# q and k of all but the first half batch transposed by DMA from SBUF to SBUF instead of on TensorE

## The chip, the cores and the metric

One core of one Trainium2 chip. The metric is the device time of one execution in microseconds (us). The kernel before takes 264.52 us (median of 4 runs, 264.51 to 264.59). A run is repeated on the same chip beside runs of the kernel before.

## The reference

A sparse attention (4 batches, 8 heads, 768 positions, head size 64) followed by two products with a gated activation between them:

```python
k_sum = k.reshape(B, H, nb, 32, D).max(axis=3)       # one summary key per block of 32
v_sum = v.reshape(B, H, nb, 32, D).mean(axis=3)
scores_l = where(|i - j| < 16, scale * q @ k.T, -1e9) # a narrow band
scores_s = scale * q @ k_sum.T + log(32)              # and the 24 summaries
a = softmax(concat(scores_l, scores_s)); attn = a @ concat(v, v_sum)
h = x @ w_in                                          # x: 3072 x 512, w_in: 512 x 2048
out = (h * sigmoid(1.702 * h)) @ w_out                # w_out: 2048 x 512
```

## The kernel before

The work runs in eight half batches of 384 positions. Each has a first product (tile `ph`, into `gT`) and a second one (tile `po`). Attention for the next half batch is interleaved with the second product: scores (`ps_s`), values (`ps_av`), the transposition of the result (`ps_x`). The inputs of the next batch are prepared in the odd half batches (u odd), in the first product. Scores need the head dimension on the partitions, so q and k have to be transposed:

```python
def load_k(b, p):                       # two heads p: rows of 768 B (three positions each)
    for half in range(2):
        sp.dma_start(out=t[:, half]..., in_=k[b, 2*p:2*p+2, half*HALF:...].rearrange("h (p r) d -> p h (r d)", r=JH))
def cast_k(eng, p): ...                 # f32 -> bf16 on GpSimd, tile kb, three buffers
def tk(p, s, own=dve):                  # on TensorE: matmul with the identity
    for half in range(2):
        p3 = big[:, half*512:half*512+HALF].rearrange("p (c r) -> p r c", r=JH)   # columns written with a step of 3
        for r in range(JH):
            pe.matmul(out=p3[:, r], lhsT=src[:, half, r]..., rhs=ident, start=True, stop=True)
    # DVE: copy from PSUM into the key tile kx, block maxima ks, 16-column halos
def tq(p, half, e0, e1):                # the same for q: 3 matmuls, two DVE copies into zero-padded qz
    ...
# an odd half batch (u odd): what GpSimd casts for the next batch, and the slots of the first product
todo = {1: [tk(0)], 2: [tk(1)], 4: [vsum(0,1,2)], 5: [vsum(3,4,5), vrows], 6: [tk(2)], 8: [tk(3)],
        9: [tq(0,0)], 11: [tq(1,0)], 12: [tq(2,0)], 14: [tq(3,0)]}
cast_k(pool, 0); cast_k(pool, 1)
for j in range(NJ): cast_v(pool, s, j, 0); cast_v(pool, s, j, 1)     # twelve v casts
cast_k(pool, 2); cast_q(pool, 0, 0)                                  # the fourth k cast follows at slot 2
# an even half batch: tq(p, 1) at slots 3, 6, 9, 12; the next batch's loads are issued in its second product
```

`vsum` sums v by blocks on TensorE from cast v, `vrows` then copies rows within `vw` by six DMAs. Each engine, and SyncE's queue of DMA instructions, works strictly in program order. [...]

The softmax here doesn't subtract the row's maximum and nothing guards it: scores larger than these inputs give would overflow.

## Time and profile before

| | before |
|---|---|
| time | 264.52 us |
| TensorE busy | 89% |
| from one odd half's end to the next | 56.8 us |
| an odd half (31 us) is longer than an even one (26 us) by | 4.8 us, the preparation of the next batch |

How to read such a page: a row of 40 digits is the span in 40 slices, 9 is 90% busy or more; `PEclk` is the granted clock in tenths. TensorE at 9 all along with no waits is the bound. The lines are shown in the prediction below. Lines in order of time have the start and the length in us, the engine, the operation, the tiles written and read, and in brackets how long the engine stood idle before and for whom. `SPq` is SyncE's queue of DMA instructions; its length there is how long the instructions held the queue, not how long the data took to land. A "slot" is one of the sixteen column blocks of the first product.

### The profile page before, as it was taken

How to read it: one execution, taken by the hardware profiler on the slowest of the kernel's cores; microseconds unless marked ns; L12 is line 12 of the kernel's file. 1: busy time of each engine (PE TensorE's matmuls, PEld its weight loads, DVE VectorE, ACT ScalarE, POOL GpSimd, SP SyncE). 2: the span in 40 equal slices, each digit the busy share in tenths (PEclk: the TensorE clock that was granted, in tenths of full speed). 3: DMA queues.
4: the chain of work that ended last, by engine and by line, in shares of the span. 5: the costliest groups of instructions: out<-in, count | busy, mean ns of one | idle time of the engine just before them, and what ended most of it. 6: DMA issues, size and time to landing. Idle time of an engine off the chain costs nothing.

```text
span 263.1 us, 4275 instructions
## 1 busy us (share of the span) xinstructions
PE 234.2 (89%) x1571; PEld 142.0 (54%) x1592; DVE 146.7 (56%) x336; ACT 131.3 (50%) x218; POOL 75.5 (29%) x185
## 2 busy tenths in 40 slices
PE   2543749999998999999989999999989999999994
PEld 1131535656665555655665656566656556555541
DVE  4527471447699483358796754276995745372000
ACT  3524443663644627752646446844446366637711
POOL 8890792735203003840202006820220000000000
PEclk9998555999999999999999999999999999999999
DMA  6969999998432118993150129972130210011012
GB/s 176 227 173 178 306 202 196 196 221 259 171 52 55 40 42 223 229 272 117 42 103 0 42 92 249 261 239 83 22 81 2 81 40 2 9 71 42 0 40 81
DMA packets 52981, 32.34 MB, mean 123 GB/s; under 512 B 26848, under 2 KB 49888, under 8 KB 52960
## 3 DMA queue, kind: packets, MB, share of 16 engines
q1 hardware_dynamic: 48736, 27.88, 41.9%
q0 software_dynamic: 4224, 4.19, 9.7%
q8 instruction: 12, 0.20, 0.3%
q14 instruction: 9, 0.07, 0.1%
HBM read 27.26 MB, written 6.29 MB: 128 GB/s over the span
## 4 chain that ended last, share of the span: by engine, by line
PE 74%; DVE 8%; POOL 6%; ACT 5%; DMA 2%; issue 2%; SPq 1%; ACTq 0%; POOLq 0%
PE po L27 29%; PE ph L27 26%; PE ps_s L27 4%; PE ps_q L27 4%; PE ps_av L27 4%; DVE kx L27 4%; PE ps_x L27 3%; DMA qf<-in_q_dram 2%; PE ps_k L27 2%; DVE ks L27 2%; ACT L27 2%; DVE x_sb L27 2%; PE ps_vs L27 1%; POOL qz L27 1%; POOL vw L27 1%
## 5 line engine op out<-in xcount | busy, mean ns | idle before, releaser
L27 PE MATMUL ph<-xT,w_in_sb 128*128 128x384 bf16 x512 | 97.7, 335 | 0.7 <-ACT gT L27 0.7
L27 PE MATMUL po<-w_out_sb,gT 128*128 128x512 bf16 x363 | 92.5, 379 | 0.8
L27 ACT ACTIVATE gT<-ph 128x384 bf16<-128x384 f32 x128 | 61.6, 490 | 46.3 <-PE ph L27 45.7
L27 PEld LDWEIGHTS <-w_in_sb 128*128 128x128 bf16 x512 | 52.6, 106 | 31.2 <-issue 5.2
L27 PEld LDWEIGHTS <-gT 128*128 128x128 bf16 x384 | 34.6, 97 | 28.0
L27 DVE CAST qz<-ps_q 64x384 bf16<-64x384 f32 x56 | 31.1, 555 | 28.6 <-PE ps_q L27 28.0
L27 POOL CAST qb<-qf 128x384 bf16<-128x384 f32 x32 | 16.1, 513 | 101.5 <-PE ps_q L27 63.6
L27 DVE TENSOR_TENSOR a_sb<-a_sb,mk 128x768 bf16<-128x768 bf16 x32 | 18.4, 575 | 33.8 <-ACT a_sb L27 32.9
L27 ACT ACTIVATE a_sb<-ps_s 128x768 bf16<-128x768 f32 x32 | 25.2, 809 | 23.4 <-PE ps_s L27 23.3
L27 DVE TENSOR_TENSOR x_sb<-ps_av,rc 64x384 bf16<-64x384 f32 x64 | 35.5, 555 | 1.5
L27 ACT ACTIVATE osb<-po 128x512 f32<-128x512 f32 x24 | 14.3, 597 | 41.1 <-PE ps_x L27 23.3
L27 DVE CAST kx<-ps_k 128x768 bf16<-128x768 f32 (+1 forms) x64 | 25.5, 439 | 10.3 <-PE ps_k L27 10.3
L27 POOL CAST vw<-vf 128x512 bf16<-128x512 f32 x42 | 24.6, 620 | 7.5 <-DMA vf<-in_v_dram 7.3
L27 PE MATMUL ps_k<-ident,kb 128*128 128x128 bf16 x96 | 15.5, 351 | 7.6 <-DVE kb L27 3.9
L27 POOL CAST kb<-kf 128x384 bf16<-128x384 f32 x26 | 13.5, 542 | 29.2 <-PE ps_k L27 26.5
L27 ACT ACT_TABLE_LOAD x16 | 20.5, 1283 | 1.1 <-PEq L511 0.8
L27 PE MATMUL ps_q<-ident,qb 128*128 128x128 bf16 x96 | 16.7, 316 | 4.6 <-DVE kx L27 3.4
L27 PE MATMUL ps_s<-qz,kx 128*128 128x128 bf16 x192 | 16.8, 227 | 4.3 <-ACT qz L27 4.3
L27 PEld LDWEIGHTS <-kx 128*128 128x128 bf16 x192 | 13.9, 102 | 10.4 <-issue 4.1
L27 PEld LDWEIGHTS <-a_sb 128*128 128x128 bf16 x192 | 14.4, 102 | 7.7 <-DVE a_sb L27 0.8
L27 PE MATMUL ps_av<-vw,a_sb 128*128 128x130 bf16 x192 | 17.6, 231 | 0.6 <-DVE a_sb L27 0.5
L27 PEld LDWEIGHTS <-kb 128*128 128x128 bf16 x96 | 11.2, 139 | 11.8 <-POOL kb L27 4.4
(42 smaller groups left out, 115.0 us busy)
## 6 DMA issues: line engine op xcount, KB each, us to landing
kf<-in_k_dram SPq DMA_DIRECT2D x32, 192.0 KB, 4.0
vf<-in_v_dram SPq DMA_DIRECT2D x24, 256.0 KB, 5.1
qf<-in_q_dram SPq DMA_DIRECT2D x32, 192.0 KB, 4.2
out_dram<-osb SPq DMA_DIRECT2D x24, 256.0 KB, 2.0
w_in_sb<-in_moe_w_in_dram POOLq DMA_DIRECT2D x4, 512.0 KB, 10.0
w_out_sb<-in_moe_w_out_dram POOLq DMA_DIRECT2D x4, 512.0 KB, 20.5
vw<-vs SPq DMA_DIRECT2D x8, 148.5 KB
vw<-vw SPq DMA_DIRECT2D x8, 99.0 KB, 2.9
```

What stands on the lines that cost most here:

```text
L27: r = f(*a, **kw)
```

## The change

Its intent: take the transpositions off TensorE, which is the bound, and their evacuation off DVE. GpSimd casts k and q to bf16, and the DMA engines transpose from SBUF to SBUF on the way into the key tiles and the zero-padded queries. k and q have to be loaded with positions in partitions in order, hence in 256 B rows.

```diff
+        else:
+            for hh in range(2):          # load_k, load_q of later batches: 256 B rows
+                sp.dma_start(out=t[:, hh]..., in_=k[b, 2 * p + hh].rearrange("(j p) d -> p j d", p=128))
+    qs = [keep.tile([128, JH, 2, 128], BF16, name=f"qs{i}") for i in range(3)]   # zero-padded staging
+    def turn_k(p, s):
+        t = castp.tile([128, NJ, 2, D], BF16, name="kb", tag="kb")               # three buffers
+        pool.tensor_copy(out=t..., in_=raw["k", p]...)
+        for e in range(2):
+            todo_sp.append(lambda e=e: sp.dma_start(out=k4[:, :, e, e * 64:e * 64 + 64],
+                in_=src[e * 64:e * 64 + 64], transpose=True))
+    def turn_q(p, half):
+        t = qs[qn[0] % 3]; qn[0] += 1
+        for hh in range(2):
+            pool.tensor_copy(out=t[:, :, hh, hh * 64:hh * 64 + 64], in_=raw["q", p, half][:, hh])
+        todo_sp.append(lambda: sp.dma_start(out=qz[p][half]..., in_=t..., transpose=True))
+    def rest_k(p, s): ...                # DVE: block maxima and halos, now from the key tile itself
[...]
         if half == 0:
-                cast_q(pool, p, 1)
-                todo[3 + 3 * p] = [lambda p=p: tq(p, 1, dve, dve)]
+                todo[2 + 3 * p] = [lambda p=p: turn_q(p, 1)]
         elif b + 1 < B:
-            [...]  cast_k(pool, 0), cast_k(pool, 1), v casts, cast_k(pool, 2), later cast_k(pool, 3)
+            for p in range(NP):
+                turn_k(p, s)
             for j in range(NJ):
                 cast_v(pool, s, j, 0)
                 cast_v(pool, s, j, 1)
+            todo = {4: [lambda: rest_k(0, s)], 6: [...], 8: [...], 10: [...],
+                    9: [lambda: vsum(s, (0, 1, 2)), lambda: turn_q(0, 0)],
+                    11: [lambda: vsum(s, (3, 4, 5)), lambda: vrows(s), lambda: turn_q(1, 0)],
+                    12: [lambda: turn_q(2, 0)], 13: [lambda: turn_q(3, 0)]}
         for nt in range(NT):
             ff_in(u, nt)
+            if todo_sp:
+                todo_sp.pop(0)()         # one transposing DMA behind each column block
```

## The prediction

> **What bounds the kernel now.** I read the page from the top: busy shares, the 40 slices, the chain that ended last. Then the table of busy times over stages that I cut at the chain's own boundaries, and last the lists in order of time of SyncE, GpSimd and TensorE for one batch.
>
> ```profile
> PE 234.2 (89%) x1571; PEld 142.0 (54%) x1592; DVE 146.7 (56%) x336; ACT 131.3 (50%) x218; POOL 75.5 (29%) x185
> PE   2543749999998999999989999999989999999994
> POOL 8890792735203003840202006820220000000000
> PEclk9998555999999999999999999999999999999999
> DMA  6969999998432118993150129972130210011012
> PE 74%; DVE 8%; POOL 6%; ACT 5%; DMA 2%; issue 2%; SPq 1%; ACTq 0%; POOLq 0%
> ```
>
> After about 40 us TensorE is at 9 in nearly every slice with the clock fully granted: from there on TensorE is the bound, and GpSimd and the DMA engines have bursts once per batch. The kernel runs eight half batches. I call one "even" (first half of a batch) or "odd" (second half); each has a first product (tile ph) and a second (po). In the table by stages (columns: length, then PE, PEld, DVE, ACT and POOL busy) the pair of one batch is:
>
> ```profile
> 98.50:111.00 12.50, 12.34 (x80) 7.74 (x79) 4.80 (x9) 9.11 (x18) 7.27 (x14) 1.00 1.00 219
> 111.00:124.60 13.60, 13.30 (x106) 7.96 (x107) 8.66 (x19) 6.07 (x9) 3.91 (x7) 1.00 0.67 206
> 124.60:141.40 16.80, 16.04 (x109) 10.47 (x107) 14.61 (x33) 8.99 (x17) 3.75 (x8) 1.00 0.26 57
> 141.40:155.30 13.90, 13.60 (x107) 8.09 (x109) 9.28 (x21) 6.17 (x9) 0.14 (x1) 1.00 0.10 39
> ```
>
> PE is busy 12.34 of 12.50 and 16.04 of 16.80: nothing waits long. The period is 12.5 + 13.6 + 16.8 + 13.9 = 56.8 us. The odd first product is 4.3 us longer than the even one because TensorE transposes the next batch's k and q there. How the inputs arrive (lists in order of time: SyncE's queue, then GpSimd):
>
> ```profile
> 99.43 2.00 SPq L27 DMA_DIRECT2D kf<-in_k_dram  x4
> 101.47 6.54 SPq L27 DMA_DIRECT2D vf<-in_v_dram  x6
> 108.11 2.56 SPq L27 DMA_DIRECT2D kf<-in_k_dram  x4
> 110.71 5.69 SPq L27 DMA_DIRECT2D qf<-in_q_dram  x8
> 116.49 8.93 SPq L27 DMA_DIRECT2D out_dram<-osb  x3
> 131.34 2.64 SPq L27 DMA_DIRECT2D vw<-vw  x4
> 134.09 1.71 SPq L27 DMA_DIRECT2D vw<-vs  x2
> ...
> 106.07 7.07 POOL L27 CAST vw<-vf 128x512 bf16<-128x512 f32 x12 [0.69 <-DMA vf<-in_v_dram]
> 126.89 0.51 POOL L27 CAST kb<-kf 128x384 bf16<-128x384 f32 x1 [10.39 <-PE ps_k L27]
> ```
>
> SyncE starts the next batch's loads at 99.43, right after the last output store of the odd half: it runs ahead of TensorE. Its last output store of the even half is out at about 125.4. The v casts are done by 113, long before the sums need them at 129. The last line matters most: the fourth cast of k waited 10.39 us, because the pool of cast buffers has three and the first comes free only when it has been read.
>
> **What the Trainium skill says.** "DMA: Bandwidth & Descriptors", DMA Transpose (X-bar): the plain transpose is issued by SyncE or ScalarE only and writes SBUF; the trace of before has none, so it neither agrees nor disagrees. The same page, Latency and other measured facts: 261 GB/s effective for one transposing kernel. "VectorE: DVE Perf Modes", The three transpose paths: 1309 ns by DMA for 128x128 bf16, 390 ns on TensorE. The trace differs for TensorE: six k transposes take 0.66 us of the chain and three q transposes 0.49, so 0.11 to 0.16 us each. The same DMA page, Specifications: 512 B is the least run for full rate. The trace agrees mildly: v (256 B runs) came at 1.57 MB / 6.54 us = 240 GB/s, q (768 B runs) at 1.57 / 5.69 = 276.
>
> **The change, part by part.**
> Removed from TensorE: per odd half with a next batch 4 x 0.66 (k) + 4 x 0.49 (q) = 4.6 us; per even half 4 x 0.49 = 2.0 us. Three odd and four even: 13.8 + 8.0 = 21.8 us. If nothing new showed, 264.5 - 21.8 is about 243.
> Removed from DVE: 56 casts of 0.555 us (q) and 12 of about 0.9 us (k), some 42 us. Only a few tenths per odd half lie on the chain.
> GpSimd: casts of about the same elements; little changed in amount, much in order (below).
> Loads: k and most of q now come in 256 B rows. 4.7 MB at 240 GB/s is 19.7 us instead of 17.1.
> Added: per batch 8 k transposes (64 x 768) and 8 q transposes (128 x 768) on SyncE's queue. Let T be one q transpose, and half of that for k. An estimate from the trace: 768 rows of 256 B at v's rate of 1.06 ns a row (1.09 us for 1024) is 0.8 us; the page's 261 GB/s gives 0.75. The page's 1.309 us for a sixth of the data gives 7.9, but that figure surely contains the start and the landing of one transfer (a 99 KB copy within SBUF takes 2.9 us to land here). I choose T = 1.6, twice the optimistic value, and think anything from 0.7 to 4 possible.
>
> Now the path, with the odd half's end as time 0. SyncE works in program order, and the program puts four q transposes before the loads. The zero-padded staging tiles are three, so the fourth transpose waits for a first landing and a cast: loads start near 7. They last 20 and end at 27 (the stores end at about 24.5). Only then come the k transposes. The fourth k cast now stands **before** the twelve v casts on GpSimd, and it needs the first cast buffer, hence the first pair's k transposes: 27 + 2 x 0.8 + 3.5 to land behind the loads = 32.1; its cast 33.1; v casts 7.1, so 40.2. Before, the v casts overlapped the loads. TensorE reaches the v sums at about 32 in the odd first product and stalls up to 40.2. Then 0.65 (sums) and four column blocks 2.6: the second product starts at 43.5. The row copies of v (six DMAs, 4.4 us of SyncE's queue) start at about 41.5 and stand before the second q transpose: it lands at 45.9 + 1.6 + 2 = 49.5, while the second group of scores is due at 45.6: 3.9 us more. The half ends at 43.5 + 14.1 + 3.9 = 61.5, against 56.8: about +5 per batch, although TensorE has 6.6 us less to do.
> Sum: the first half batch -2; the first odd half about +4.5, for its loads wait behind q transposes that wait for GpSimd's casts at 39 us, while before they began at 26; two full pairs 2 x 5; the seventh half -2. Together about +10: **274 us**.
>
> **The rivals.** (1) The transposes hide and TensorE stays the bound: about 243. For it: 50% DMA idle time in the slices and the small TensorE waits. Against it: the idle DMA time comes where SyncE's order cannot use it, and the 10.39 us wait for a cast buffer shows the dependency already there. If the v casts are not held up I would be wrong here.
> (2) Transposes at the bandwidth limit, T = 0.8: the loads end near 25, the v casts at 37.5, the half at about 58: +1.5 per batch, 268 in all. So even fast transposes give almost nothing, since the order of the v casts costs what TensorE saves.
> (3) SyncE's queue or the DMA engines become the bound: T = 3 costs some 5.5 us per us of T and batch (four before the loads, two k halves, one q): 274 + 1.4 x 5.5 x 3 = 297; T = 8 would give over 350. For it: 1309 ns for one block on the page. Against it: the same page's bandwidth.
> (4) TensorE's stalls cool its clock: the slices with PEclk 5 lie where it idled early. It would add one or two us per batch; I leave it inside the range.
>
> **Range and chances.** T below 0.7: 15%, to 266; 0.7 to 1.3: 25%, 266 to 272; 1.3 to 2: 25%, 272 to 283; 2 to 4: 20%, to 317; above: 15%. One chance in ten that the cast order costs less than I think moves some weight under 259. Hence 274, range 255 to 320; faster 0.13, same 0.23, slower 0.64. The result is lopsided: a gain is capped at 21.8 us, a loss is not.
>
> **What would show it.** Right: TensorE's matmuls from cast q and k drop from 192 to 36 and its busy time by about 20 us; the v casts of each batch move from the even half into the odd first product, after a GpSimd wait on a DMA; TensorE waits for v casts at the sums (several us) and for q tiles at the second scores; SyncE's loads start some 6 to 7 us after the last odd store; the row copies of v stand between the first and second q transposes. Wrong: TensorE still at 9 in all slices after 40 us (rival 1), or SyncE's queue busy without a pause and transposes taking 3 us or more each (rival 3). What would make the number wrong first is T, then how long the 256 B loads last, then whether the first k transposes really have to wait for all loads to be issued.

## The result, and the profile after

The changed kernel takes 300.03 us (median of 4 runs, 299.28 to 300.79), against 264.52. The ratio is 1.134 (95% interval 1.131 to 1.137). The time lies within the predicted range, but the forecast was +10 us and +35 came.

The page of the changed kernel (busy shares, TensorE, granted clock and DMA by slices, the chain by engine):

```profile
PE 231.7 (78%) x1415; PEld 129.9 (44%) x1436; DVE 113.0 (38%) x268; ACT 131.3 (44%) x218; POOL 74.2 (25%) x199
PE   3544679998066599999658499999568599999995
PEclk9996559999759689999959799999958599999999
DMA  6969999999744506899846614899645513201001
PE 61%; SPq 9%; POOL 9%; DMA 8%; ACT 7%; issue 3%; DVE 1%; POOLq 0%; ACTq 0%
```

TensorE has three holes after 65 us, with slices of 5 to 8 in the clock row beside them: one per odd half that prepares a batch. Its busy time fell by only 2.5 us (234.2 to 231.7) although 156 matmuls have gone. In the pair shown below it fell where the clock was full (even first product, 12.34 to 10.94 us) and not in the odd half (29.6 and 29.7 us), where the clock was 0.87 to 0.89. The chain that ended last now has SyncE's queue, GpSimd and DMA with 26% together, where before they had 9%.

I cut the span at ScalarE's change of function at the end of each half (its table load), which gives lengths that can be compared run by run:

| | first half | first odd | second odd | third odd | each even | span |
|---|---|---|---|---|---|---|
| before | 68.2 | 30.8 | 30.8 | 30.8 | 26.0 | 263.1 |
| after | 67.0 | 48.4 | 41.5 | 42.6 | 24.7 | 298.1 |

The even halves gained 1.3 us each, as work left TensorE. The three odd halves lost 17.6, 10.8 and 11.8. The stages of the pair that answers to the one shown before (same columns):

```profile
114.70:125.80 11.10, 10.94 (x68) 6.47 (x68) 0.36 (x1) 9.02 (x17) 0.64 (x2) 1.00 0.84 153
125.80:139.40 13.60, 13.30 (x104) 7.82 (x105) 8.61 (x19) 6.10 (x8) 2.48 (x3) 1.00 1.31 213
139.40:167.80 28.40, 16.89 (x86) 8.61 (x87) 10.48 (x23) 11.60 (x20) 10.07 (x21) 0.87 0.68 142
167.80:181.00 13.20, 12.83 (x91) 7.39 (x92) 8.03 (x18) 3.62 (x5) 1.94 (x6) 0.89 0.20 59
```

In the third row TensorE is busy 16.89 of 28.40 us, at a granted clock of 0.87. SyncE's queue over this pair (in order of time; the even half begins at 114.8, the odd one at 139.6):

```profile
115.82 6.02 SPq L27 DMA_TRANSPOSE qz<-qs  x4
121.89 2.37 SPq L27 DMA_DIRECT2D kf<-in_k_dram  x4
...
134.97 9.69 SPq L27 DMA_DIRECT2D qf<-in_q_dram  x16
...
146.25 10.37 SPq L27 DMA_TRANSPOSE kx<-kb  x8
158.45 1.21 SPq L27 DMA_TRANSPOSE qz<-qs  x1
159.75 2.61 SPq L27 DMA_DIRECT2D vw<-vw  x4
162.46 1.70 SPq L27 DMA_DIRECT2D vw<-vs  x2
164.26 4.07 SPq L27 DMA_TRANSPOSE qz<-qs  x3
```

The loads begin 7 us after the odd half's end, behind four q transposes; they end at 144.7; eight k transposes hold the queue for 10.4 us; the last three q transposes stand behind the row copies of v. GpSimd in the same odd half:

```profile
150.16 0.83 POOL L27 CAST kb<-kf 128x768 bf16<-128x768 f32 x1 [12.44 <-DMA kx<-kb]
150.93 6.91 POOL L27 CAST vw<-vf 128x512 bf16<-128x512 f32 x12
```

And TensorE:

```profile
151.63 0.58 PE L27 MATMUL ps_vs<-vw,E 128*128 128x512 bf16 x1 [4.97 <-POOL vw L27]
154.30 2.77 PE L27 MATMUL ph<-xT,w_in_sb 128*128 128x384 bf16 x8
...
157.62 2.76 PE L27 MATMUL ph<-xT,w_in_sb 128*128 128x384 bf16 x16
...
167.93 0.80 PE L27 MATMUL ps_s<-qz,kx 128*128 128x128 bf16 x6 [4.79 <-DMA qz<-qs]
168.52 2.98 PE L27 MATMUL po<-w_out_sb,gT 128*128 128x512 bf16 x8
```

The fourth k cast waited 12.44 us for the first k transposes to land, and only then come the v casts. TensorE waits 4.97 us for the first of them, and 4.79 us for the second q tile. After the first wait 8 matmuls of the first product take 2.77 us, as long as 16 of them three microseconds later: the clock was at half.

And the first odd half, which lost most. SyncE's queue in the half before it:

```profile
37.56 13.49 SPq L27 DMA_TRANSPOSE qz<-qs  x4
51.10 4.48 SPq L27 DMA_DIRECT2D kf<-in_k_dram  x4
```

GpSimd meanwhile:

```profile
48.17 0.64 POOL L27 CAST qs<-qf 128x192 bf16<-128x192 f32 x2 [9.51 <-issue]
```

The first batch's four q transposes hold the queue for 13.49 us, because they land 10.5 to 14.9 us after issue while the weights are being loaded, and the fourth has to wait for a staging tile: its cast comes at 48.17. (The profile names no releaser for that cast, "issue"; that it is the first of the three staging tiles follows from the program.) The loads of the second batch start at 51.10; before they started at 26.13. The start overstates the delay, though, for in the kernel before the v loads then stood in the queue for 23.69 us beside the weights:

```profile
28.82 23.69 SPq L27 DMA_DIRECT2D vf<-in_v_dram  x6
```

So the loads ended at 64.0 before and at 75.9 after: 12 us later, not 25.

### The profile page after: what moved, and what is told of

The parts are those of the page before. It is cut to its first block, busy times and chain, and to the rows that moved or that the text cites. A ratio compares the mean times of both kernels' runs of the same rounds, so it can differ in the third digit from the quotient of the medians.

```text
span 298.1 us, 4015 instructions
## 1 busy us (share of the span) xinstructions
PE 231.7 (78%) x1415; PEld 129.9 (44%) x1436; DVE 113.0 (38%) x268; ACT 131.3 (44%) x218; POOL 74.2 (25%) x199
## 3 DMA queue, kind: packets, MB, share of 16 engines
HBM read 27.26 MB, written 6.29 MB: 113 GB/s over the span
## 4 chain that ended last, share of the span: by engine, by line
PE 61%; SPq 9%; POOL 9%; DMA 8%; ACT 7%; issue 3%; DVE 1%; POOLq 0%; ACTq 0%
PE po L27 25%; PE ph L27 23%; SPq L27 9%; POOL vw L27 4%; PE ps_av L27 4%; PE ps_s L27 4%; DMA qz<-qs 4%; PE ps_x L27 3%; ACT L27 3%; DMA kx<-kb 3%; ACT osb L27 2%; DMA qf<-in_q_dram 2%; PE ps_vs L27 2%; ACT gT L27 1%; POOL qz L27 1%
## 5 line engine op out<-in xcount | busy, mean ns | idle before, releaser
L27 PE MATMUL po<-w_out_sb,gT 128*128 128x512 bf16 x363 | 97.6, 395 | 0.8
L27 PE MATMUL ph<-xT,w_in_sb 128*128 128x384 bf16 x512 | 94.0, 341 | 1.1 <-ACT gT L27 1.0
L27 PEld LDWEIGHTS <-gT 128*128 128x128 bf16 x384 | 36.0, 101 | 31.0 <-issue 5.3
L27 POOL CAST qs<-qf 128x192 bf16<-128x192 f32 x56 | 17.5, 353 | 81.0 <-DMA qz<-qs 63.7
L27 POOL CAST kb<-kf 128x768 bf16<-128x768 f32 (+1 forms) x14 | 11.2, 806 | 86.9 <-DMA kf<-in_k_dram 42.4
L27 PE MATMUL ps_vs<-vw,E 128*128 128x512 bf16 x24 | 12.1, 549 | 26.2 <-POOL vw L27 23.1
L27 PEld LDWEIGHTS <-kx 128*128 128x128 bf16 x192 | 14.5, 105 | 27.1 <-issue 21.3
L27 DVE TENSOR_REDUCE ks<-kx 128x24 bf16<-128x768 bf16 x12 | 11.4, 951 | 36.4 <-DMA kx<-kb 36.3
L27 PEld LDWEIGHTS <-E 128*128 128x128 bf16 x24 | 2.9, 121 | 30.2 <-issue 30.0
L27 PE MATMUL ps_x<-ident,x_sb 128*128 128x128 bf16 x96 | 11.2, 229 | 3.2 <-DVE xT L27 3.2
L27 DVE COPY xT<-ps_x 128x384 bf16<-128x384 bf16 x32 | 11.4, 358 | 4.3 <-PE ps_x L27 3.5
```

What stands on the lines that cost most here:

```text
L27: r = f(*a, **kw)
```

## The experiments

The theories. **Order**: what costs is the place of things in two in-order queues, GpSimd's (the v casts behind a k cast that waits for a transpose) and SyncE's (loads behind q transposes, row copies behind k transposes, q transposes behind row copies). **Transpose time**: the transposes in themselves are too slow or fill the DMA engines. **Small rows**: the 256 B loads cost. **Clock**: TensorE's stalls cool it. Lengths of odd halves are of the profiled runs, at the same cuts as above.

**e1: four k cast buffers instead of three.**

```diff
+    kbp = ctx.enter_context(tc.tile_pool(name="kbp", bufs=4))
-        t = castp.tile([128, NJ, 2, D], BF16, name="kb", tag="kb")
+        t = kbp.tile([128, NJ, 2, D], BF16, name="kb4", tag="kb4")
```

> The changed kernel with four k cast buffers instead of three, nothing else. Theory CAST ORDER (my prediction's main step: the fourth k cast holds the v casts back until the first k transposes have landed, and that is what costs): the v casts go back beside the loads, the stall of TensorE at the v sums (5 to 10 us per odd half with a next batch) goes, and the time falls by some 8 us per odd half, to 270-278 us. Theory QUEUE ORDER (the queue of SyncE is the real chain: loads, eight k transposes of 1.25 us, then row copies of v and q transposes, and the cast order only lies in its shadow): the stall moves from the v sums to the first two groups of scores, and the time falls by only 2 to 4 us per odd half, to 288-294 us.

295.45 us, ratio to the kernel before 1.117. TensorE in the second odd half:

```profile
145.18 0.81 PE L27 MATMUL ps_vs<-vw,E 128*128 128x512 bf16 x3
...
158.50 0.80 PE L27 MATMUL ps_s<-qz,kx 128*128 128x128 bf16 x6 [7.10 <-DMA qz<-qs]
...
165.12 0.80 PE L27 MATMUL ps_s<-qz,kx 128*128 128x128 bf16 x6 [4.11 <-DMA qz<-qs]
```

The v sums wait for nothing any more, and the wait stands again before the first scores (7.10 us) and the second (4.11). Only 4.6 us came back, a little less than the queue theory's range allowed (288 to 294): the cast order that my prediction called the main step lies in the shadow of SyncE's queue.

**e2 and e3: one part of the change alone.** In e2 only k goes by DMA; q is loaded, cast and transposed on TensorE as before. In e3 it is the reverse: k as before, with the v casts in their old place.

```diff
 # e2                                              # e3
-    turn_q(p, half) everywhere                    -    turn_k(p, s), rest_k(p, s)
+    cast_q(pool, p, half); tq(p, half, dve, dve)  +    cast_k(pool, p); tk(p, s) at slots 1, 2, 6, 8
                                                   +    vsum at slots 4 and 5, as before
```

> k by DMA as in the change, q of all batches loaded, cast and transposed on TensorE as before. Theory QUEUE/CAST ORDER: the loads start right at the end of the odd half again (no q transposes ahead of them), the k transposes start at the last store of the even half, some 24 us after the odd half's end, the v sums still wait 2 to 4 us and no scores wait for q: 262-268 us. Theory TRANSPOSE TIME (the 24 k transposes and their packets cost in themselves, about half of the loss): about 280 us.

277.69 us, ratio 1.050; the odd halves take 34.9 to 35.2 us. A miss for the order theory's numbers; it lies near the rival's "about 280". One new wait, which neither theory had, makes up nearly all of the loss (12.2 us in the three odd halves), on TensorE in the second odd half:

```profile
140.96 0.82 PE L27 MATMUL ps_q<-ident,qb 128*128 128x128 bf16 x3 [4.08 <-POOL qb L27]
```

The q casts stand on GpSimd behind the v casts, which still stand behind the fourth k cast, so now TensorE waits for a cast q.

> q by DMA as in the change, k loaded, cast and transposed on TensorE as before, so the v casts run beside the loads as before. Theory ORDER: the v sums wait for nothing from the second batch on, the q transposes come after the row copies of v well before the scores; TensorE is rid of 4 x 0.49 us in seven half batches; 250-260 us, with some loss only in the first odd half, where the loads wait for the q transposes of the first batch. Theory TRANSPOSE TIME: q has 28 of the 52 transposes and the larger ones, so half or more of the 35 us loss stays: 280 us or more.

256.32 us, ratio 0.969: faster than the kernel before, with 28 of the 52 transposes, and the larger ones. The odd halves take 33.2, 28.3 and 29.2 us. Only the first shows the late loads. This speaks against transpose time as the cause for q: more than half of the transposes are there and the loss is not. For k it says nothing.

**e4: the kernel before with 256 B loads.** k and q loaded as in the change, transposed on TensorE; each transposing matmul then writes contiguous PSUM columns.

```diff
 # load_k, load_q: two DMAs with 256 B rows in place of one [...]
-  p3 = ps.rearrange("p (c r) -> p r c", r=JH)      # the same for k
+  p3 = ps.rearrange("p (r c) -> p r c", r=JH)
```

> The kernel before, with k and q loaded in 256 B rows as the change does (twice the load instructions for both) and transposed on TensorE; only the order of columns within the transposes differs. Theory ORDER: the loads last 3 to 5 us longer per batch, nothing waits for it, 263-267 us. Rival SMALL ROWS (the smaller rows are what costs): 272 us or more.

259.51 us, ratio 0.981. Unforeseen, this is faster: the odd halves take 29.9 us. It is taken up in e11. Small rows cost nothing that shows here, where nothing waits for the loads. That doesn't clear them in the change: a batch's loads held the queue 17.0 us before (second pair), 24.7 in e4 and 22.8 in the change (of the 5.8 us more, q's loads take 4.0, in 16 instructions instead of 8), and there the transposes stand behind them. No run tests the change with its small rows taken away.

**e5: no q transposes in front of the loads.** The first batch's second-half q goes over TensorE again; those of later batches are issued in the preceding odd half.

```diff
         if half == 0:
-            todo[2 + 3 * p] = [lambda p=p: turn_q(p, 1)]
+            for p in range(NP) if b == 0 else ():
+                cast_q(pool, p, 1); todo[3 + 3 * p] = [lambda p=p: tq(p, 1, dve, dve)]
[...]
+        if half == 1 and b + 1 < B:
+            for p in range(NP): turn_q(p, 1)
```

> The changed kernel with the q transposes of second halves taken from in front of the loads: those of the first batch are done on TensorE again (as in the kernel before), those of later batches are issued in the preceding odd half, behind the first half's. Nothing else. Theory QUEUE ORDER (the loads of a batch wait in SyncE's queue behind four q transposes: 7 us per batch, and some 20 us in the first odd half, where these wait in turn for staging tiles and land late beside the weights): loads start right at the odd half's end, the k transposes start at the even half's last store instead of 6 us later; the first odd half gets 10 to 14 us shorter, the two later ones about 5 us each; 276-283 us. Rival BANDWIDTH (the loads and the weights fill the DMA engines anyway, in whatever order): the first odd half stays within 4 us of its 48 us, 290 us or more.

283.06 us, ratio 1.069. The odd halves take 40.4, 37.0 and 36.6 us: 8.0 less than in the changed kernel in the first, 4.5 and 6.0 in the others. So this place in the queue was worth 17 of the 35 us, just short of the 276 to 283 expected; the first odd half missed the 10 to 14 us expected of it. SyncE's queue in the half before it:

```profile
26.40 4.92 SPq L27 DMA_DIRECT2D kf<-in_k_dram  x4
31.36 25.48 SPq L27 DMA_DIRECT2D vf<-in_v_dram  x6
```

The loads begin 24.7 us earlier than in the change but end only 5.7 us earlier (70.2 against 75.9), as the v loads stand in the queue beside the weights again. So the rival's number (within 4 us of 48) is refuted, but not that what runs beside the weights is slow in whatever order.

**e6: two q transposes in one instruction.**

```diff
-  sp.dma_start(out=qz[p][half]...,  in_=t..., transpose=True)     # 128 x 768
+  sp.dma_start(out=qzp[pp][half]..., in_=t..., transpose=True)    # 128 x 1536, two head pairs
```

> The changed kernel with two q transposes in one instruction (128x1536 instead of twice 128x768), to measure what holds the queue: theory HOLD PER SIZE: one takes 2.4 to 2.6 us of SyncE's queue, twice the 1.24 of a single one. Rival HOLD PER INSTRUCTION: still 1.2 to 1.5 us. By its making the second q of a first half is no longer behind the row copies of v, so the wait of the second scores (4 to 6 us per odd half) should go either way: 284-292 us with the first theory, 280-286 with the second.

289.38 us, ratio 1.093. What one transpose holds of the queue (ns, least, median, most) and how long it takes to land (us), for q of the changed kernel, then its k, then the merged q of e6:

```profile
L27 SPq DMA_TRANSPOSE qz<-qs x28: 1211/1239/5205, 37.6 to 253.4; - x28
DMA to landing us min/median/max: 2.7/3.0/14.9
```

```profile
L27 SPq DMA_TRANSPOSE kx<-kb x24: 1208/1248/1367, 77.9 to 221.5; - x24
DMA to landing us min/median/max: 2.4/2.5/3.1
```

```profile
L27 SPq DMA_TRANSPOSE qz<-qs x14: 1415/1596/7156, 39.2 to 239.4; - x14
DMA to landing us min/median/max: 3.8/4.3/5.3
```

The time lies in the first theory's range, the hold in neither's: half a q (k, 64x768) holds the queue as long as a q (1.25 and 1.24 us), and two q in one hold it 1.6 us. In these shapes the hold is mostly per instruction. Back to back, four q take 5.25 us, which is 786 KB at 150 GB/s; two merged ones take 3.35, which is 235 GB/s; eight k take 10.37 for 786 KB, 76 GB/s. The transposes as the change has them use the queue badly, and k worst.

**e7: idle matmuls in TensorE's waits.**

```diff
+    def warm(ps):                     # ahead of the first v sum and of the second scores of odd halves
+        for i in range(18):
+            pe.matmul(out=ps, lhsT=ident, rhs=w_out_sb[:, i % NT, :], start=True, stop=True)
```

> The changed kernel with 18 matmuls of no use put ahead of the first v sum and ahead of the second group of scores of each odd half, where TensorE stands idle 5 to 10 us; they fill about 4 us of that wait and change nothing else. Theory CLOCK (the clock granted after each stall is lower, and the matmuls that follow run at half speed for 2 to 3 us, which is 3 to 4 us per odd half of the 35 us lost): 289-295 us, granted clock in the odd first products above 0.95. Rival NO CLOCK EFFECT (the chain runs through the queue and the casts, and slower matmuls lie in its shadow): 298 us or more.

292.92 us, ratio 1.106, in the clock theory's range. TensorE at the second scores of the second odd half, after the idle matmuls:

```profile
164.57 0.49 PE L27 MATMUL ps_s<-qz,kx 128*128 128x128 bf16 x6 [1.38 <-DMA qz<-qs]
164.90 1.89 PE L27 MATMUL po<-w_out_sb,gT 128*128 128x512 bf16 x8
```

The same eight matmuls took 2.98 us in the changed kernel. 7.1 us, or 2.4 per odd half, came back though nothing was taken away. The clock was thus a part of the loss and not in another chain's shadow. The granted clock, cut at the start of the second product, rose to 1.00 in the three second products (from 0.86, 0.92 and 0.84). In the first products it rose only to 0.86, 0.92 and 0.92 (from 0.78, 0.84 and 0.76), where above 0.95 was expected: there TensorE still waited for v casts, up to 6.29 us. The Trainium skill, "TensorE: Matmul & The Clock Gate", Part 1, says that the clock halves after an idle window of about 3.4 us; the traces agree for the six long waits of the changed kernel (4.54 to 9.80 us), each followed by slowed matmuls; a wait of 2.5 us in e12 below was followed by slow matmuls once and once not.

**e8: only q by DMA, both chains avoided.** k over TensorE with contiguous writes, q transposes of both halves in the odd half, the first half's ahead of the row copies, none ahead of the loads, four k cast buffers.

```diff
+            cast_k(pool, 0) ... v casts ... cast_k(pool, 2); cast_k(pool, 3)
+            for p in range(NP): turn_q(p, 0)
+            todo = {1: [tk(0, s)], 2: [tk(1, s)], 4: [vsum(s, (0, 1, 2))],
+                    5: [vsum(s, (3, 4, 5)), vrows(s)], 6: [tk(2, s)], 8: [tk(3, s)]}
+            # turn_q(p, 1) at slots 9 to 12
```

> Only q by DMA, k of later batches on TensorE from rows loaded as in e4 (contiguous writes to PSUM), q transposes of both halves issued in the odd half, the first half's ahead of the row copies of v, none ahead of the loads, four k cast buffers. Theory ORDER: no stall of TensorE over 1 us after 40 us; its work falls by 28 - 4 q transposes (24 x 0.49 = 12 us) and by 12 x 0.27 = 3 us for k; 245-252 us, faster than the kernel before and than e3 and e4. Rival TRANSPOSE TIME: the DMA engines are too full and it is no better than e3 (256 us).

250.99 us, ratio 0.948. Its page, busy shares and TensorE by slices:

```profile
PE 224.1 (90%) x1520; PEld 131.3 (53%) x1520; DVE 122.3 (49%) x288; ACT 131.2 (53%) x218; POOL 83.0 (33%) x215
PE   2635576999999899999999999999999999999994
```

From 44 us to the last slice TensorE is at 9, but for one slice of 8: the odd halves take 27.0 us (28.0 the first).

**e9: e2 with four k cast buffers.**

```diff
+    kbp = ctx.enter_context(tc.tile_pool(name="kbp", bufs=4))
-        t = castp.tile(..., name="kb", tag="kb")
+        t = kbp.tile(..., name="kb4", tag="kb4")
```

> e2 (only k by DMA, 277.7 us) with four k cast buffers. In the full change the fourth buffer gave only 5 us, since SyncE's queue lay right behind. Here no q transposes stand in that queue. Theory TWO CHAINS (cast order and queue order each hold TensorE up by themselves, so taking one away helps only where the other is absent): the v casts go back beside the loads, TensorE waits for nothing over 1 us in the odd first products, and the time falls by 20 us to 253-259 us, under the kernel before. Rival TRANSPOSE TIME (k transposes of 10.4 us per batch on the queue cost in themselves): 268 us or more.

268.51 us, ratio 1.013 (0.997 to 1.029). A miss again: 9 us less than e2, where 20 were expected, and the time lies in the rival's range (268 or more). TensorE in the first odd half:

```profile
82.44 0.61 PE L27 MATMUL ps_q<-ident,qb 128*128 128x128 bf16 x3 [3.33 <-DVE qz L27]
```

The v sums wait for nothing, as expected, but now TensorE waits 3.33 us for DVE's copy of a transposed q: DVE, also in order, stands at the block maxima of a key tile that a transpose has still to deliver. That is a third in-order queue on which the change put a wait for a transpose. The lesson for the theory: two chains were too few. With k alone by DMA, order and the 10.4 us that its transposes hold per batch were not separated.

**e10: all by DMA, both chains cut.** Two head pairs per instruction for k and q, a cast buffer for each, order in the queue: k, q, k, q (first half), row copies, q (second half), and loads free of q transposes; v sums at slots 2 and 3.

```diff
+            turn_k(0, s); [v casts]; turn_q(0, 0); turn_k(1, s); turn_q(1, 0)     # merged pairs
+            todo = {2: [vsum(s, (0, 1, 2))], 3: [vsum(s, (3, 4, 5)), vrows(s)], 4: [rest_k(0, s)],
+                    5: [rest_k(1, s)], 6: [rest_k(2, s)], 8: [rest_k(3, s)], 9: [turn_q(0, 1)], 10: [turn_q(1, 1)]}
```

> All of k and q of later batches by DMA as the change meant it, but with both chains cut: two heads' pairs in one transposing instruction (half as many), a cast buffer for each, second-half q issued in the odd half and not ahead of the loads, the first-half q transposes and all k transposes ahead of the row copies of v, the v sums early. Theory ORDER: 243-251 us, at or under e8 (251.0), with TensorE's odd half at about 26 us. Rival BANDWIDTH/HOLD (the queue and the DMA engines have no room for all transposes, loads and copies within a batch): 255 us or more.

261.99 us, ratio 0.988 (0.977 to 0.999). The kernel is back at the time of the one before, with 48 of the change's 52 transposes still made by DMA (in 24 instructions; the first batch's four q are on TensorE): the 35 us were lost by order, cast buffers and the number of instructions, which e10 changes together, and not by these transposes as such. But it missed the 243 to 251 expected and lies in the rival's range (255 or more). Where it stuck (TensorE, first odd half):

```profile
89.80 0.77 PE L27 MATMUL ps_av<-vw,a_sb 128*128 128x130 bf16 x6 [5.14 <-DMA vw<-vs]
```

**e11: the kernel before with contiguous PSUM writes**, 256 B rows from the second batch on, no DMA transpose.

```diff
+  if b == 0: [...]                                        # rows of 768 B as before
+  else: sp.dma_start(out=t[:, hh], in_=q[b, 2 * p + hh, ...].rearrange("(j p) d -> p j d", p=128))
+  p3 = (ps.rearrange("p (r c) -> p r c", r=JH) if rows else ps.rearrange("p (c r) -> p r c", r=JH))
```

> The kernel before with k and q of later batches (not the first) loaded in 256 B rows and transposed on TensorE into contiguous PSUM columns: no DMA transpose at all. Theory: the three q matmuls take 0.33 instead of 0.49 us and the six k matmuls about 0.4 instead of 0.66, together some 7 us; 255-260 us. It tells how much of e8's gain comes from the DMA transposes and how much from this. Rival: e4's gain came from something else in its order, and this is 262 us or more.

260.68 us, ratio 0.983, just over the range. The transposing matmuls of q in the kernel before and in e11 (ns, least, median, most):

```profile
L27 PE MATMUL ps_q<-ident,qb x96: 269/314/502, 21.6 to 222.1; 128*128 128x128 bf16 x96
```

```profile
L27 PE MATMUL ps_q<-ident,qb x96: 216/219/502, 21.6 to 217.8; 128*128 128x128 bf16 x96
```

A transposing matmul that writes every third column takes 314 ns, one that writes them side by side 219. So some 4 us of e8's 13.5 are not the DMA's doing; against e11 the q transposes by DMA, with e8's order and its fourth k cast buffer, are worth 9.7 us (260.68 - 250.99; the runs are of different rounds).

**e12: e10 with loads moved.** The second half's q is loaded behind the row copies, and transposed behind the odd half's first store. **e13** is e8 once more, unchanged, timed beside it.

```diff
-                for p in range(NP): load_q(b + 1, p, 1)          # with the other loads
+   slot 3: [vsum(s, (3, 4, 5)), vrows(s)] + [load_q(b + 1, p, 1) for p in range(NP)]
-   slots 9, 10: turn_q(0, 1), turn_q(1, 1)
+            if half == 1 and b + 1 < B and i == 5:               # in the second product
+                turn_q(0, 1); turn_q(1, 1)
```

> e10 (all by DMA, merged, 262.0 us) with the loads of the second-half q moved from in front of the k transposes to behind the row copies of v, and their transposes behind the odd half's first store. In e10 SyncE's queue is busy without a pause for 44 of the 58 us of a batch and TensorE waits 5 us per odd half for the row copies, at the queue's end. Theory QUEUE ORDER: the row copies come 4 to 5 us earlier, this wait goes, 244-250 us. Rival BANDWIDTH (the DMA engines are full, whatever the order): 256 us or more.

> e8 once more, word for word, timed in three rounds beside e12 and the kernel before: 250-252 us. It does not test a theory; it tells whether the version with k on TensorE or the one with everything by DMA is the better.

e12: 256.20 us, ratio 0.967 (0.963 to 0.970); e13: 251.62, ratio 0.950 (0.948 to 0.952). The order theory had the direction again, and 5.8 us came by moving the second half's q, loads and transposes, but it was at the rival's edge (256 or more). The wait for the row copies is halved, not gone (TensorE, second odd half of e12):

```profile
139.44 0.51 PE L27 MATMUL ps_av<-vw,a_sb 128*128 128x130 bf16 x6 [2.49 <-DMA vw<-vs]
```

With everything by DMA, SyncE's queue stays the second bound. The best version is e8: k on TensorE, q by DMA, 5% under the kernel before.

| time, us | first odd | second odd | third odd | |
|---|---|---|---|---|
| before 264.52 | 30.8 | 30.8 | 30.8 | |
| after 300.03 | 48.4 | 41.5 | 42.6 | |
| e1 295.45 | 47.2 | 40.8 | 40.5 | fourth k cast buffer |
| e5 283.06 | 40.4 | 37.0 | 36.6 | loads not behind q transposes |
| e6 289.38 | 44.9 | 37.5 | 37.4 | two q per instruction |
| e7 292.92 | 45.2 | 39.6 | 40.4 | clock kept up |
| e2 277.69 | 34.9 | 34.9 | 35.2 | k alone |
| e9 268.51 | 32.8 | 33.3 | 31.1 | k alone, fourth buffer |
| e3 256.32 | 33.2 | 28.3 | 29.2 | q alone |
| e10 261.99 | 32.7 | 30.3 | 28.6 | all, merged and reordered |
| e12 256.20 | 28.5 | 30.0 | 27.9 | and loads moved |
| e8 250.99 | 28.0 | 27.0 | 27.1 | q alone, reordered, k contiguous |

## Why the prediction was right or wrong

**The waits were right.** Loads 7 us after the odd half's end, behind the four q transposes; the fourth k cast waiting for the first transposes; the v casts moved behind it; TensorE waiting at the v sums and at the second scores; the row copies between the first and second q transposes: each is in the trace as named, and the matmuls from cast q and k did drop from 192 to 36. One sign failed: TensorE's busy time was to fall by about 20 us and fell by 2.5, for what the odd halves no longer do is made up by matmuls at the lower clock. "Even fast transposes give almost nothing" was never tested as put: q's held the queue shorter than chosen and 35 us were lost all the same, but merging them (e6), which also took the second q from behind the row copies, gave 10.7 us.

**The sum was mis-sized, +10 where +35 came.** By the prediction's own terms, in the cuts of the table:

| term | predicted | measured |
|---|---|---|
| first half and three even halves | -2.0 each | -1.2 and -1.3 |
| first odd half | +4.5 | +17.6 |
| second and third odd half (5 per pair, with an even half's -2) | +7 each | +10.8, +11.8 |

*The first odd half* is the term that failed worst, 13 of the 25 us. "Its loads wait behind q transposes that wait for GpSimd's casts at 39 us" named a wait and gave it less time than the later halves got. The first three casts were done by 38.7, but the transposes landed up to 14.9 us after issue beside the weights, and the staging tile made the fourth wait for a landing; the loads began at 51. e5 took the transposes away from there: 8.0 us of this half came back. The other 9.6 are more than the later halves still lose in e5 (6.2 and 5.8); there the loads end at 70.2, against 64.0 before, beside the weights. That their v loads stand there for some 25 us, in the kernel before too, the prediction did not see; it looked only at when the loads began.

*The pairs* missed 4.5 and 5.5 us. The first of them shows where. Counted from the odd half's end (114.7): the loads ended at 30.0 and not 27 (22.8 us for the 20 estimated); a k transpose held 1.25 us and not 0.8, for the hold is mostly per instruction and not per byte (e6); the row copies began at 45.1, not 41.5, behind eight k transposes and a q one; the second q landed at about 53.2, not 49.5; the half ended at 66.3, not 61.5, so the last 1.2 us of the miss came after the second scores began, at the lower clock. T for q was 1.24 to 1.31 us, **below** the 1.6 chosen. And the clock, "one or two us per batch; I leave it inside the range", was worth some 2.4 us per odd half (e7, which did not cure all of it) and belonged in the sum.

*The gain on TensorE* was over-counted. The pieces of the chain (0.49 us for three q matmuls) include the last one's modelled end; from start to start three take 0.30 us (in the odd first product of before, 135.09 to 135.39). Four of them make 1.2 us per even half, and 1.3 were gained, not 2.0. For the same reason the "0.11 to 0.16 us each" set against the page's 390 ns is a pace and not a length: one such matmul's record lasts 314 ns in the trace of before (e11).

*The range* was not one sum either: by the 5.5 us per us of T and batch of rival (3), T = 4 gives 314 us and not 317, and T = 0.8 gives 261 where rival (2) says 268.

**The main step was not the main step.** The prediction called the cast order decisive. e1 shows that mending it alone gives 4.6 us, because SyncE's queue stands right behind; e5 shows 17 us for one place in the queue. The rival "transposes hide" is wrong for the change as written. For q alone it is right once the order is mended (e8). What stays open: e10 and e12 show that the queue is still what TensorE waits for when everything goes by DMA, but not whether an order exists that hides it all; the DMA engines' own load was never separated from the queue's; for k, transpose time was not separated from order (e2, e9); and what the small rows cost in the change, where they hold the queue longer, was not tested.

## What to carry to other kernels

Moving work from a busy engine to an idle one adds waits to every in-order queue that issues, feeds or consumes it; walk each of these queues (here SyncE, GpSimd and DVE) in program order before counting the gain, and give every item that is named as a delay a time of its own. Put transfers that others wait for ahead of those with slack, merge small transposing DMAs, and move only the part that fits: q alone, reordered, gained 5% (with k's contiguous writes, some 4 us of it) where q and k together as written lost 13%. When one wait is taken away and little comes back, look for the wait that took its place.

## What the Trainium skill lacked or had wrong

- "DMA: Bandwidth & Descriptors" (DMA Transpose) does not say, shape by shape, how long a transpose within SBUF holds the issuing queue on this chip: here 1.25 us for 64x768, 1.24 for 128x768, 1.6 for 128x1536.
- "Advanced Engine Details and Errata", X-Bar Transpose, says that transposes are as fast as regular DMAs, 350 to 400 GB/s. Here back-to-back transposes of 98 to 393 KB were issued at 76 (64x768), 150 (128x768) and 235 GB/s (128x1536): only the largest comes near the loads' 240.
- "VectorE: DVE Perf Modes", The three transpose paths, gives 1309 ns by DMA for 128x128. Six such blocks in one instruction landed in 3.0 us and twelve in 4.3, so the figure does not scale by blocks.
- "TensorE: Matmul & The Clock Gate", Part 1, ties the halved clock to an idle window of about 3.4 us. In e12 a wait of 2.49 us was followed by four matmuls of the second product in 1.91 us instead of 1.03; after one of 2.60 us they were not slowed. Idle time that short is not safe.
- "SBUF — State Buffer" (Door 1: The DMA port swizzle) says that a non-contiguous PSUM pattern slows matmuls significantly, but not by how much: the transposing matmul with a step of three took 314 ns in the trace, without it 219, and three of them 0.30 against 0.17 us from start to start.
